# Two experts' last 64 query rows in one 128-row tile, and a sign bit placed by the activation that rescales a weight

## The chip, the cores and the metric

The kernel runs on one core of one Trainium2 chip. TensorE (PE) multiplies matrices, VectorE (DVE), ScalarE (ACT) and GpSimd (POOL) work element by element, and SyncE (SP) issues most DMA transfers. Each engine takes its own instructions strictly in the order of the program; semaphores hold one back until its inputs are there. The metric is device time of one execution in microseconds (us).

## The reference, cut to what matters

Four batches of 576 positions go through three stages in float32.

```python
# 1. sparse attention: 8 heads, 4 local (32 back), 4 strided (every 32nd)
scores = where(mask, q @ k.T / 8, -1e9); attn = softmax(scores); x = attn @ v     # (4, 576, 512)
# 2. token-shift MLP; w_k (512 x 1024), w_v (1024 x 512), w_r (512 x 512) come as float64
k = maximum(xk @ w_k, 0); v = (k * k) @ w_v; x = sigmoid(xr @ w_r) * v
# 3. dense causal attention, one head (d = 64) for each of 4 experts, weighted by a top-2 gate
for e in range(4):
    a = softmax(where(causal, -1e9, scale * (x @ wq[e]) @ (x @ wk[e]).T))
    out += gate[e] * (a @ (x @ wv[e]) @ wo[e])
```

## The kernel before, in words

Matrices are multiplied as sums of high and low parts (`split`): three products for a full-precision one, in the type F32R, which TensorE reads in one pass. Transposes and the products with the attention weights are plain float32.

**The float64 weights.** The three MLP matrices come as raw 64-bit words, in 20 pieces of 128 x 512 (`weight_units`, four of `w_r`, eight of `w_k`, eight of `w_v`). Each piece is turned to float32 by integer steps: a DMA loads the words; `scale` (ACT, L165 and L167) takes the upper words as float32 numbers and multiplies them by 2^-112, which moves the exponent to where float32 wants it, and turns the lower words to an integer; `shift` (DVE, L171) moves the upper words left by 3 bits, which drops their sign; `add` (DVE, L174) adds the low bits; `sign` (DVE, L177) takes the sign bit from the upper word and puts it into the result; `high` (ACT, L184) and `low` (DVE, L188) split the result into its parts. `w_r` needs no split in the first batch.

**Stage order.** `first_batch` is written out by hand and pinned: in ten steps it interleaves the sparse attention of batch 0 with pieces 0 to 5. Then come the gate products of batch 0 (TensorE, L526, plain float32), and a loop in which pieces 7 to 19 are made. Its last eight passes each hold one group of 12 TensorE products (`mm1`, L506 to L508, tile `pk`), whose result ACT takes out of PSUM (L510), squares (L514) and rounds (L117), and DVE completes (L120). `pk` has three PSUM buffers, shared with the gate products, which ACT copies out at L532. The rest of batch 0 and batches 1 to 3 follow, with the next batch's sparse attention between the MLP products.

**The dense attention.** For each batch `proj_units` makes queries `Q`, keys `KH`, `KL`, values `V` and gate weights `gw`; `attn_tiles` cuts the 576 query rows into five tiles of 128 (the last one, t = 4, holds 64 real rows; its upper 64 partitions read whatever stands behind). The batch's second chunk (tiles 2, 3, 4) comes first, then the first (tiles 0, 1). For each tile and expert `sc` makes the scores (two products each for up to 512 keys; tile 4 has 576 keys, so two parts of 288), DVE adds the mask and finds the row's extreme (L1027), ACT takes the exponential with the row's sum (L1033). `norm` makes one factor for a row (L1041 to L1043), `trp` multiplies by it (DVE, L1048), transposes in blocks of 128 keys on TensorE (L1058, tile `pt`, two PSUM buffers), and ACT copies the blocks out (L104, tile `aT`). `av` multiplies with the values (L1080, `py`), `wout` with the output weights (L1096 to L1098, `pw`), and SP stores the result. The work of one batch is interleaved by planned costs with the projections of the next, and outside the pinned part a scheduler with a time model decides each engine's final order, so the order on the chip is fixed beforehand.

Of the kernel before, what the change touches and what calls it, by code (L numbers as in the profile page):

```python
# [7 lines left out]
F32 = mybir.dt.float32  # L8
F32R = mybir.dt.float32r
# [33 lines left out]
def kernel(  # L43
# [100 lines left out]
    def weight_units():  # L144
        units = []

        def piece(dst_h, dst_l, src, early=True):
# [42 lines left out]
            return dict(load=load, scale=scale, shift=shift, add=add, sign=sign, high=high, low=low)  # L190
# [428 lines left out]
    def first_batch():  # L619
# [10 lines left out]
        def w(j, what):  # L630
            if 0 <= j < NW:
                wu[j][what]()
# [11 lines left out]
        def pieces(j, extra=()):  # L644
# [5 lines left out]
            w(j, "sign")  # L650
# [90 lines left out]
        w(6, "sign")  # L741
# [141 lines left out]
    nc.sync.dma_start(mcau, c_cau)  # L883
    tri = p3.tile([P, E, E], F32, tag="tri", name="tri", bufs=1)
# [3 lines left out]
    def proj_units(b):  # L888
        units = []

        Qf = p3.tile([P, E * S + P // 2], F32R, tag="Q", name=f"Q{b}")
        nc.gpsimd.memset(Qf[:, E * S:].bitcast(F32), 0.0)
        Q = Qf[:, :E * S].rearrange("p (e s) -> p e s", e=E)
# [4 lines left out]
        pst[b] = dict(Q=Qf, KH=KH, KL=KL, V=V, gw=gw)  # L898
        nc.gpsimd.memset(V[64:P, NT - 1, :], 0.0)
        for ci, (s0, N) in enumerate(CHUNKS):  # L900
# [41 lines left out]

            for ep in range(EP):
                units.append(qkp(True, ep))
                units.append(qkp(False, ep))

# [16 lines left out]
        def gate():  # L963
# [21 lines left out]
            nc.vector.tensor_tensor(gw, gw, mx.unsqueeze(2).to_broadcast([P, NT, E]), op=ALU.mult)  # L985

# [3 lines left out]
    def attn_tiles(b):  # L990

        res = []
        Q, KH, KL, V, gw = (pst[b][n] for n in ("Q", "KH", "KL", "V", "gw"))
        for ci, (s0, N) in reversed(list(enumerate(CHUNKS))):
# [4 lines left out]
            def tile_units(t, ci=ci, s0=s0, N=N, nkt=nkt, cst=cst):  # L999


                m = P
                mq = min(P, S - t * P)
                nk = min(S, (t + 1) * P)
                nkp = (t + 1) * P
                st = {}

                def sc(e):
                    def f():
# [3 lines left out]
                        pe = p3.tile([P, nkp], F32, tag=f"pe{t}", name=f"pe{b}_{t}_{e}", bufs=4)  # L1013
                        st["p", e] = pe
                        if nkp > nk:
                            nc.gpsimd.memset(pe[:, nk:], 0.0)
                        qs = Q[:, e * S + t * P:e * S + t * P + m]
                        parts = [(0, nk)] if nk <= 512 else [(0, 288), (288, nk - 288)]
                        nm, sm = st["nm"], st["sm"]
                        for i, (c0, n) in enumerate(parts):  # L1020
                            pm = ps_sc(f"s3_{b}_{t}_{e}_{i}")
                            nc.tensor.matmul(pm[:m, :n], qs, KH[:, e, c0:c0 + n], start=True, stop=False)  # L1022
                            nc.tensor.matmul(pm[:m, :n], qs, KL[:, e, c0:c0 + n], start=False, stop=True)  # L1023

                            mo = 384 - (t * P - c0)
                            mask = mcau[:m, mo:mo + n] if c0 + n > t * P else mcau[:m, :n]
                            nc.vector.tensor_tensor_reduce(  # L1027
                                out=pe[:m, c0:c0 + n], in0=pm[:m, :n], in1=mask,
                                scale=-0.125, scalar=(BIG if i == 0 else nm[:m, 2 * e:2 * e + 1]),
                                op0=ALU.add, op1=ALU.min, accum_out=nm[:m, 2 * e + i:2 * e + i + 1],  # L1030
                            )
                            last = nm[:m, 2 * e + i:2 * e + i + 1]
                        nc.scalar.activation(  # L1033
                            pe[:m, :nk], pe[:m, :nk], AF.Exp, bias=last, scale=-1.0,
                            accum_out=sm[:m, e:e + 1],
                        )
                    return (0.6, f)

                def norm():
                    sm = st["sm"]  # L1040
                    nc.vector.tensor_scalar_add(sm[:m, :], sm[:m, :], 1e-9)  # L1041
                    nc.vector.reciprocal(sm[:m, :], sm[:m, :])
                    nc.vector.tensor_tensor(sm[:m, :], sm[:m, :], gw[:m, t, :], op=ALU.mult)  # L1043

                def trp(e):
                    def f():
                        pe = st["p", e]
                        nc.vector.tensor_scalar_mul(pe[:m, :nk], pe[:m, :nk], st["sm"][:m, e:e + 1])  # L1048
                        if ("aT", e) not in cst:
                            cst["aT", e] = p3.tile([P, nkt, N], F32, tag=f"aT{ci}", name=f"aT3_{b}_{ci}_{e}", bufs=4)  # L1050
                        aT = cst["aT", e]
                        qo = t * P - s0
                        for k0 in range(0, t + 1, 4):
                            kn = min(4, t + 1 - k0)
# [170 lines left out]
```

## Time and profile before

| | us |
|---|---|
| median of 3 runs (lowest, highest) | 577.26 (576.7, 579.78) |
| the profiled execution, its own time | 578.21 |
| its span, first to last instruction | 576.3 |
| busy: PE / DVE / ACT / POOL | 550.2 / 391.2 / 336.2 / 94.8 |

The granted TensorE clock is 1.00 over the whole span. In a row, "x" is a count, "busy, mean ns" the time and mean duration of a group, and "[a <-b]" says that the engine sat idle for a us and that b ended it. Matmuls are pipelined: a new one starts before the last one's modelled end, so the distance between two starts is the cost of one, and a busy PE can still be late.

### The profile page before, as it was taken

The page shows a single profiled execution, that of the slowest core. Times are in us where ns is not written, and L with a number is a line of the kernel's source. Part 1 is how long each engine was busy: PE and PEld are TensorE (multiplying, and loading weights), DVE is VectorE, ACT ScalarE, POOL GpSimd, SP SyncE. Part 2 cuts the span into 40 slices and gives each one's busy share as a digit, 9 for nine tenths or more (in the row PEclk, how much of TensorE's full clock was granted, in tenths as well). Part 3 has the DMA queues.
Part 4 walks back from the last instruction along what each step waited for, and adds up shares of the span by engine and source line. Part 5 has one row for each costly group of instructions (what it writes and reads, how often), then busy time and mean ns, then how long its engine had stood idle before and what let it go on. Part 6 is the DMA issues. An engine that isn't in the chain of part 4 may idle for free.

```text
span 576.3 us, 12027 instructions
## 1 busy us (share of the span) xinstructions
PE 550.2 (95%) x4408; PEld 497.8 (86%) x4408; DVE 391.2 (68%) x1350; ACT 336.2 (58%) x994; POOL 94.8 (16%) x147
## 2 busy tenths in 40 slices
PE   4889889989999999999999999999999999999987
PEld 3657789879999998999999999999978998898956
DVE  3897998867975465964465943246888865875862
ACT  4987878780455351445453753157776864775763
POOL 0000000101211121301022000076513242220000
PEclk9999999999999999999999999999999999999999
DMA  8962431234002305001203230055502250321102
GB/s 266 339 248 82 142 137 35 85 119 142 2 1 77 99 17 189 2 19 70 88 11 96 79 100 30 30 113 107 123 16 57 65 129 6 79 46 37 61 23 83
DMA packets 26367, 49.70 MB, mean 86 GB/s; under 512 B 3524, under 2 KB 20676, under 8 KB 25540
## 3 DMA queue, kind: packets, MB, share of 16 engines
q1 hardware_dynamic: 21188, 44.21, 23.1%
q0 software_dynamic: 5120, 4.72, 4.6%
q8 instruction: 34, 0.56, 0.4%
q14 instruction: 25, 0.20, 0.1%
HBM read 34.77 MB, written 9.44 MB: 77 GB/s over the span
## 4 chain that ended last, share of the span: by engine, by line
PE 76%; DVE 10%; ACT 5%; issue 2%; DVEq 0%; ACTq 0%
PE pk L506 6%; PE pv L563 6%; PE pk L507 5%; PE pk L508 5%; PE pv L565 5%; PE pv L564 5%; PE py L1080 4%; PE pt L1058 4%; PE pr L542 2%; PE pr L543 2%; PE pr L544 2%; PE s L1022 2%; PE pos L413 2%; PE s L1023 2%; PE pw L1096 2%; PE ss L382 2%
## 5 line engine op out<-in xcount | busy, mean ns | idle before, releaser
L506 PE MATMUL pk<-xh,wkh 128*128 128x320 f32 (+1 forms) x256 | 79.1, 310 | 3.8 <-ACT rf L510 2.8
L563 PE MATMUL pv<-kk,wvh 128*128 128x320 f32 (+1 forms) x256 | 76.5, 303 | 0.0
L507 PE MATMUL pk<-xl,wkh 128*128 128x320 f32 (+1 forms) x256 | 75.3, 294 | 0.0
L508 PE MATMUL pk<-xh,wkl 128*128 128x320 f32 (+1 forms) x256 | 75.2, 294 | 0.0
L564 PE MATMUL pv<-kk,wvh 128*128 128x320 f32 (+1 forms) x256 | 74.4, 294 | 0.0
L565 PE MATMUL pv<-kk,wvl 128*128 128x320 f32 (+1 forms) x256 | 74.0, 294 | 0.0
L1033 ACT ACTIVATE pe<-pe,nm 128x384 f32<-128x384 f32 (+4 forms) x80 | 48.3, 606 | 12.5 <-DVE nm L1027 10.2
L510 ACT ACTIVATE rf<-pk 128x320 f32<-128x320 f32 (+1 forms) x64 | 26.0, 405 | 49.9 <-PE pk L508 46.3
L506 PEld LDWEIGHTS pk<-xh,wkh 128*128 128x128 f32 x256 | 48.0, 188 | 7.8 <-ACT rf L510 3.8
L237 ACT ACTIVATE el<-el,nm 128x96 f32<-128x96 f32 x72 | 26.2, 365 | 45.2 <-DVE nm L232 44.7
L563 PEld LDWEIGHTS pv<-kk,wvh 128*128 128x128 f32 x256 | 47.7, 188 | 2.1 <-issue 0.3
L507 PEld LDWEIGHTS pk<-xl,wkh 128*128 128x128 f32 x256 | 48.1, 188 | 0.1
L508 PEld LDWEIGHTS pk<-xh,wkl 128*128 128x128 f32 x256 | 48.1, 188 | 0.1
L564 PEld LDWEIGHTS pv<-kk,wvh 128*128 128x128 f32 x256 | 47.9, 188 | 0.0
L565 PEld LDWEIGHTS pv<-kk,wvl 128*128 128x128 f32 x256 | 47.8, 188 | 0.1
L1027 DVE CUSTOM_DVE_ANT_0 pe<-s,mcau 128x384 f32<-128x384 f32 (+4 forms) x80 | 36.6, 480 | 10.4 <-PE s L1023 9.7
L104 ACT COPY aT<-pt 128x256 f32<-128x256 f32 (+3 forms) x96 | 33.4, 381 | 16.2 <-PE pt L1058 15.5
L1058 PE MATMUL pt<-ident,pe 128*128 128x128 f32 x240 | 37.9, 276 | 2.1 <-ACT aT L104 1.3
L568 DVE TENSOR_TENSOR sg<-pv,sg 128x320 f32<-128x320 f32 (+1 forms) x32 | 14.4, 456 | 35.6 <-PE pv L565 32.2
L120 DVE TENSOR_TENSOR kk<-rf,kk 128x320 fp32r<-128x320 f32 (+1 forms) x64 | 31.2, 488 | 4.6 <-ACT kk L117 3.4
L237 ACT ACTIVATE es<-es,nm 108x108 f32<-108x108 f32 (+1 forms) x80 | 30.3, 383 | 6.6 <-DVE nm L232 6.5
L1022 PE MATMUL s<-KH,Q 128*128 128x288 f32 (+4 forms) x96 | 31.9, 342 | 1.1 <-DVE nm L1027 1.1
(163 smaller groups left out, 1553.6 us busy)
## 6 DMA issues: line engine op xcount, KB each, us to landing
qkv<-in_loc_dram SPq DMA_DIRECT2D x6, 1168.0 KB, 5.2
qkv<-in_strd_dram SPq DMA_DIRECT2D x6, 896.0 KB, 4.7
wraw<-in_w_k_dram SPq DMA_DIRECT2D x7, 512.0 KB, 6.5
qkv<-in_w_v_dram SPq DMA_DIRECT2D x5, 512.0 KB, 4.1
x_spill<-sg SPq DMA_DIRECT2D x16, 160.0 KB, 1.8
x2f<-x_spill SPq DMA_DIRECT2D x4, 640.0 KB, 4.2
out_dram<-ot SPq DMA_DIRECT2D x16, 160.0 KB, 1.8
wraw<-in_w_r_dram SPq DMA_DIRECT2D x4, 512.0 KB, 7.7
```

The costliest lines, as they stand in the source:

```text
L104: nc.scalar.copy(dst, src)
L237: nc.scalar.activation(eg, eg, AF.Exp, bias=nm[:np_, i:i + 1], scale=-1.0, accum_out=sm[:np_, i:i + 1],)
L506: nc.tensor.matmul(pm[:, :N], wkh[:, kc, fs], xh[:, kc, :N], start=(kc == 0), stop=False)
L507: nc.tensor.matmul(pm[:, :N], wkh[:, kc, fs], xl[:, kc, :N], start=False, stop=False)
L508: nc.tensor.matmul(pm[:, :N], wkl[:, kc, fs], xh[:, kc, :N], start=False, stop=(kc == NKC - 1))
L563: nc.tensor.matmul(pm[:, :N], wvh[:, fc, os_], kh[:, :N], start=(fc == 0), stop=False)
L564: nc.tensor.matmul(pm[:, :N], wvh[:, fc, os_], kl[:, :N], start=False, stop=False)
L565: nc.tensor.matmul(pm[:, :N], wvl[:, fc, os_], kh[:, :N], start=False, stop=(fc == NFC - 1))
L1022: nc.tensor.matmul(pm[:m, :n], qs, KH[:, e, c0:c0 + n], start=True, stop=False)
L1027: nc.vector.tensor_tensor_reduce(out=pe[:m, c0:c0 + n], in0=pm[:m, :n], in1=mask, scale=-0.125, scalar=(BIG if i == 0 else nm[:m, 2 * e:2 ...
L1033: nc.scalar.activation(pe[:m, :nk], pe[:m, :nk], AF.Exp, bias=last, scale=-1.0, accum_out=sm[:m, e:e + 1],)
L1058: nc.tensor.transpose(pt[:, kk * P:(kk + 1) * P], pe[:, c0:c0 + P], ident)
```

## The change

Two parts. `sign` is gone: the activation on the upper words is Prelu instead of Copy. It multiplies a negative input by a further 2^32, which adds 32 to its exponent, so that the left shift by 3 bits moves that bit into the sign's place. And the last tile of the dense attention takes two experts at a time: 64 rows of expert 2*ep in partitions 0 to 63 and of expert 2*ep + 1 in 64 to 127. `QT` holds for a pair the first expert's query rows, 64 zero columns, and the second's; four products, two with each expert's keys, add up in one PSUM tile, and the zeros keep the experts apart.

```diff
-                nc.scalar.activation(hi.bitcast(F32), hi.bitcast(F32), AF.Copy, scale=2.0 ** -112)
+                nc.scalar.activation(hi.bitcast(F32), hi.bitcast(F32), AF.Prelu, scale=2.0 ** -112, alpha=2.0 ** 32)
...
-                nc.vector.tensor_tensor(t["w"], t["w"], t["lo"], op=ALU.add)
-
-            def sign():
-                nc.vector.scalar_tensor_tensor(
-                    dst_h if dst_l is None else t["w"], t["hi"], -0x80000000, t["w"],
-                    op0=ALU.bitwise_and, op1=ALU.bitwise_or,
-                )
+                nc.vector.tensor_tensor(dst_h if dst_l is None else t["w"], t["w"], t["lo"], op=ALU.add)
...
+    mtail = p3.tile([P, S // 2], F32, tag="mtail", name="mtail", bufs=1)
+    nc.sync.dma_start(mtail[:, :TZ], c_cau[:, :TZ])
+    for j in range(2):
+        nc.sync.dma_start(mtail[TW * j:TW * j + TW, TZ:], c_cau[:TW, 384:384 + TW])
...
-        nc.gpsimd.memset(Qf[:, E * S:].bitcast(F32), 0.0)
+        QT = p3.tile([P, EP, 3, TW], F32R, tag="QT", name=f"QT{b}")
+        nc.gpsimd.memset(QT[:, :, 1, :].bitcast(F32), 0.0)
...
+            def tails():
+                for j in range(2):
+                    nc.vector.tensor_copy(QT[:, :, 2 * j, :], Q[:, j::2, TQ:].bitcast(F32))
...
+            for j in range(2):
+                nc.vector.tensor_copy(gwt[TW * j:TW * j + TW, :], gw[:TW, NT - 1, j::2])
...
+            def tail_units(s0=s0, probs=probs):
...
+                        pe = p3.tile([P, NT * P], F32, tag=f"pe{t}", name=f"pe{b}_{t}_{ep}", bufs=3)
...
+                        for i, (c0, n) in enumerate(TPARTS):
+                            pm = ps_sc(f"s3_{b}_{t}_{ep}_{i}")
+                            for j in range(2):
+                                qs = QT[:, ep, j:j + 2, :].rearrange("p a s -> p (a s)")
+                                for h, K in enumerate((KH, KL)):
+                                    nc.tensor.matmul(
+                                        pm[:, :n], qs, K[:, 2 * ep + j, c0:c0 + n],
+                                        start=(j + h == 0), stop=(j + h == 2),
+                                    )
...
+                        for k0 in range(0, NT, 4):
+                            kn = min(4, NT - k0)
+                            pt = ps_tr(f"pt3_{b}_{t}_{ep}_{k0}")
+                            for k in range(kn):
+                                c0 = (k0 + k) * P
+                                nc.tensor.transpose(pt[:, k * P:(k + 1) * P], pe[:, c0:c0 + P], ident)
...
+                return [sc(ep) for ep in range(EP)], [(0.0, norm)] + [trp(ep) for ep in range(EP)]
```

The other tiles keep their work; the transposed weights of two experts now share one buffer (`aT`, two buffers of twice the size instead of four).

How the order moves, at the two places that matter below. First DVE in the loop over the weight pieces (L174 `add`, L188 `low`, L177 `sign`, L171 `shift`; after the change the lines are L174, L182 and L171). Before:

```order
L174 ISA wf_659<-wraw_355,wf_659 128x1024
L188 TENSOR_TENSOR wkl_76<-wf_635,wkh_75 128x512
L177 SCALAR_TENSOR_TENSOR wf_659<-wraw_355,wf_659 128x512
L171 TENSOR_SCALAR wf_669<-wraw_357 128x512
L174 ISA wf_669<-wraw_357,wf_669 128x1024
L188 TENSOR_TENSOR wkl_76<-wf_659,wkh_75 128x512
L177 SCALAR_TENSOR_TENSOR wf_669<-wraw_357,wf_669 128x512
L171 TENSOR_SCALAR wf_680<-qkv0_1_97 128x512
```

After, at the same pieces:

```order
L174 ISA wf_650<-wraw_351,wf_650 128x1024
L182 TENSOR_TENSOR wkl_76<-wf_627,wkh_75 128x512
L171 TENSOR_SCALAR wf_659<-wraw_353 128x512
L174 ISA wf_659<-wraw_353,wf_659 128x1024
L182 TENSOR_TENSOR wkl_76<-wf_650,wkh_75 128x512
L171 TENSOR_SCALAR wf_669<-qkv0_1_97 128x512
```

The row of L177 is missing once a piece and nothing else moved; a piece's value is now complete at `add`, two DVE instructions earlier.

Second, TensorE near the program's end: the transposes of the last tile of batch 3 (`pt_3_4`, then expert and first key block) among the scores of tile 1 (`s_3_1`) and the products with the values (`py_1`). Before:

```order
L1023 MATMUL s_3_1_3_0_7138<-KL_6088,Q_6085 128x256
L1058 MATMUL pt_3_4_0_0_7078<-ident,pe_4_0_6933 128x128 x4
L1058 MATMUL pt_3_4_0_4_7084<-ident,pe_4_0_6933 128x128
L1058 MATMUL pt_3_4_1_0_7088<-ident,pe_4_1_6944 128x128 x4
L1080 MATMUL py_1_0_7168<-aT_3_1_0_6888,V_6089 64x320
L1058 MATMUL pt_3_4_1_4_7094<-ident,pe_4_1_6944 128x128
L1058 MATMUL pt_3_4_2_0_7098<-ident,pe_4_2_6955 128x128 x4
```

After (expert pairs now):

```order
L1116 MATMUL pt_3_4_0_0_6956<-ident,pe_4_0_6825 128x128 x4
L1032 MATMUL s_3_1_2_6990<-KH_6015,Q_6011 128x256
L1033 MATMUL s_3_1_2_6990<-KL_6016,Q_6011 128x256
L1032 MATMUL s_3_1_3_6996<-KH_6015,Q_6011 128x256
L1033 MATMUL s_3_1_3_6996<-KL_6016,Q_6011 128x256
L1116 MATMUL pt_3_4_0_4_6962<-ident,pe_4_0_6825 128x128
L1116 MATMUL pt_3_4_1_0_6966<-ident,pe_4_1_6840 128x128 x4
L1138 MATMUL py_1_0_7024<-aT_3_1_0_6782,V_6017 64x320 x6
```

Two pairs stand where four experts stood, and the first pair's transposes moved up between the scores of tile 1.

## Rows read from the trace of the kernel before

**Rows 1.** By stretch (us): busy and count of each engine, clock, DMA.

```profile
12.00:44.70 32.70, 27.28 (x222) 19.55 (x219) 29.26 (x118) 26.88 (x97) 0.00 (x0) 1.00 0.83 305
44.70:82.00 37.30, 33.51 (x170) 27.61 (x170) 31.56 (x63) 30.12 (x62) 0.19 (x1) 1.00 0.29 90
140.00:372.00 232.00, 232.00 (x1966) 219.78 (x1965) 145.76 (x492) 101.68 (x303) 33.42 (x42) 1.00 0.17 57
372.00:548.60 176.60, 174.83 (x1336) 160.52 (x1335) 125.17 (x436) 120.47 (x341) 57.23 (x94) 1.00 0.30 70
548.60:576.00 27.40, 22.23 (x154) 16.20 (x152) 10.98 (x45) 12.35 (x44) 0.00 (x0) 1.00 0.15 49
```

**Rows 2.** Who waited for whom, TensorE, 44.7 to 82 us: total, times, longest.

```profile
PE pk L506 <- ACT rf L510: 2.8, 4, 0.9
PE pk L506 <- ACT sg L532: 1.0, 2, 0.8
```

**Rows 3.** Groups by form, line L177: busy us, mean ns.

```profile
L177 DVE SCALAR_TENSOR_TENSOR wf<-wraw,wf 128x512 int32<-128x512 int32 x10 | 6.8, 682 | 0.0
```

**Rows 4.** Who waited for whom, ScalarE, 57 to 79.3 us.

```profile
ACT wkh L184 <- DVE wf L177: 2.6, 5, 1.1
ACT wvh L184 <- DVE wf L177: 1.1, 2, 0.6
```

**Rows 5.** Timeline of VectorE in the loop over pieces: start, duration.

```profile
81.85 0.68 DVE L174 CUSTOM_DVE_ANT_0 wf<-wraw,wf 128x1024 uint16<-128x1024 uint16 x1
83.05 0.68 DVE L177 SCALAR_TENSOR_TENSOR wf<-wraw,wf 128x512 int32<-128x512 int32 x1
83.66 0.42 DVE L171 TENSOR_SCALAR wf<-wraw 128x512 int32<-128x512 int32 x1
84.39 0.68 DVE L174 CUSTOM_DVE_ANT_0 wf<-wraw,wf 128x1024 uint16<-128x1024 uint16 x1
```

**Rows 6.** Timeline of TensorE, end of batch 0's sparse attention.

```profile
38.62 0.68 PE L402 MATMUL pts<-ident,es 126*126 126x126 f32 x2 [0.55 <-DVE aTs L662]
41.79 0.79 PE L402 MATMUL pts<-ident,es 108*108 108x108 f32 x3 [0.50 <-DVE aTs L662]
```

**Rows 7.** Timeline of TensorE in the dense attention.

```profile
471.22 0.34 PE L1022 MATMUL s<-KH,Q 128*128 128x384 f32 x1
471.39 0.71 PE L1058 MATMUL pt<-ident,pe 128*128 128x128 f32 x5
471.86 0.43 PE L1023 MATMUL s<-KL,Q 128*128 128x384 f32 x1
472.12 0.31 PE L923 MATMUL pq_False<-x2h,wqh 128*128 128x320 f32 x1
```

**Rows 8.** Groups by form, dense attention, VectorE and ScalarE.

```profile
L1048 DVE TENSOR_SCALAR pe<-pe,sm 128x128 f32<-128x128 f32 x16 | 3.5, 283 | 0.1
L1027 DVE CUSTOM_DVE_ANT_0 pe<-s,mcau 128x288 f32<-128x288 f32 x16 | 7.1, 451 | 1.4 <-PE s L1023 1.2
L1027 DVE CUSTOM_DVE_ANT_0 pe<-s,mcau,nm 128x288 f32<-128x288 f32 x16 | 8.2, 513 | 2.7 <-PE s L1023 2.2
L1048 DVE TENSOR_SCALAR pe<-pe,sm 128x576 f32<-128x576 f32 x16 | 7.3, 517 | 0.1
L1033 ACT ACTIVATE pe<-pe,nm 128x576 f32<-128x576 f32 x16 | 12.5, 778 | 4.3 <-DVE nm L1027 3.9 <-DVE sm L1041 0.2
```

**Rows 9.** Timeline of TensorE near the end, batch 3.

```profile
547.64 0.29 PE L1023 MATMUL s<-KL,Q 128*128 128x288 f32 x1
551.88 0.74 PE L1058 MATMUL pt<-ident,pe 128*128 128x128 f32 x5 [0.78 <-DVE pe L1048]
555.50 0.66 PE L1058 MATMUL pt<-ident,pe 128*128 128x128 f32 x4 [0.94 <-ACT aT L104]
```

**Rows 10.** Groups by form, ScalarE: the rescaling and a table load.

```profile
L165 ACT ACTIVATE wraw<-wraw 128x512 f32<-128x512 f32 x14 | 9.4, 672 | 4.6 <-DMA wraw<-in_w_r_dram 4.6
L237 ACT ACT_TABLE_LOAD x4 | 5.1, 1283 | 4.7 <-DVE nm L232 3.9 <-PEq L1212 0.7
```

More of the change, by code (lines that the diff above doesn't have):

```diff
@@ L188, in low @@
                     nc.vector.tensor_tensor(dst_l, t["w"].bitcast(F32), dst_h.bitcast(F32), op=ALU.subtract)
-            return dict(load=load, scale=scale, shift=shift, add=add, sign=sign, high=high, low=low)
+            return dict(load=load, scale=scale, shift=shift, add=add, high=high, low=low)
         for kc in range(NKC):
@@ L649, in pieces @@
                 f()
-            w(j, "sign")
             place(j)
@@ L997, in attn_tiles, with probs, tile_units @@
             nkt = tiles[-1] + 1
[L999 to L1005, printed above, removed]
+            def probs(ep, ci=ci, N=N, nkt=nkt, cst=cst):
+                if ("aT", ep) not in cst:
+                    cst["aT", ep] = p3.tile([P, 2, nkt, N], F32, tag=f"aT{ci}", name=f"aT3_{b}_{ci}_{ep}")
+                return cst["aT", ep]
+            def tile_units(t, s0=s0, probs=probs):
+                nk = (t + 1) * P
                 st = {}
@@ L1012, in f @@
                             st["sm"] = p3.tile([P, E], F32, tag="sm3", name=f"sm3_{b}_{t}")
-                        pe = p3.tile([P, nkp], F32, tag=f"pe{t}", name=f"pe{b}_{t}_{e}", bufs=4)
+                        pe = p3.tile([P, nk], F32, tag=f"pe{t}", name=f"pe{b}_{t}_{e}", bufs=4)
                         st["p", e] = pe
[L1015 to L1032, printed above, removed]
@@ L1033, in f @@
-                        nc.scalar.activation(
-                            pe[:m, :nk], pe[:m, :nk], AF.Exp, bias=last, scale=-1.0,
-                            accum_out=sm[:m, e:e + 1],
+                        qs = Q[:, e * S + t * P:e * S + t * P + P]
+                        nm, sm = st["nm"][:, e:e + 1], st["sm"]
+                        pm = ps_sc(f"s3_{b}_{t}_{e}")
+                        nc.tensor.matmul(pm[:, :nk], qs, KH[:, e, :nk], start=True, stop=False)
+                        nc.tensor.matmul(pm[:, :nk], qs, KL[:, e, :nk], start=False, stop=True)
@@ L1036, in f @@
+                        nc.vector.tensor_tensor_reduce(
+                            out=pe, in0=pm[:, :nk], in1=mcau[:, 512 - nk:],
+                            scale=-0.125, scalar=BIG, op0=ALU.add, op1=ALU.min, accum_out=nm,
                         )
+                        nc.scalar.activation(pe, pe, AF.Exp, bias=nm, scale=-1.0, accum_out=sm[:, e:e + 1])
                     return (0.6, f)
@@ L1047, in f @@
                         pe = st["p", e]
[L1048 to L1051, printed above, removed]
+                        nc.vector.tensor_scalar_mul(pe, pe, st["sm"][:, e:e + 1])
+                        aT = probs(e // 2)[:, e % 2]
                         qo = t * P - s0
-                        for k0 in range(0, t + 1, 4):
-                            kn = min(4, t + 1 - k0)
-                            pt = ps_tr(f"pt3_{b}_{t}_{e}_{k0}")
-                            for kk in range(kn):
-                                c0 = (k0 + kk) * P
-                                nc.tensor.transpose(pt[:, kk * P:(kk + 1) * P], pe[:, c0:c0 + P], ident)
+                        pt = ps_tr(f"pt3_{b}_{t}_{e}")
@@ new lines, in f @@
+                        for k in range(t + 1):
+                            nc.tensor.transpose(pt[:, k * P:(k + 1) * P], pe[:, k * P:(k + 1) * P], ident)
+                        evac(
+                            aT[:, :t + 1, qo:qo + P],
+                            pt[:, :nk].rearrange("p (k c) -> p k c", c=P),
+                            nc.scalar,
+                        )
+                    return (0.4, f)
+                return [sc(e) for e in range(E)], [(0.0, norm)] + [trp(e) for e in range(E)]
```

65 lines of the change are left out of this document (51 added, 14 removed).

## The prediction

> **What bounds the kernel now.** I read the busy time by stretch first [rows 1], since the mean over the span (TensorE 95%) hides that the stages have different limits. From 140 to 372 us TensorE is busy the whole 232 us and VectorE 63% of it: there only TensorE counts, and neither part of the change touches it. From 372 to 548.6 us, the dense attention, TensorE is busy 174.83 of 176.6 us: a VectorE or ScalarE saving is hidden there, and only what leaves TensorE's queue pays. Before 82 us it is otherwise: from 12 to 44.7 us VectorE works 29.26 of 32.7 us and TensorE 27.28, from 44.7 to 82 us VectorE 31.56 of 37.3. And in the last 27.4 us TensorE is idle for 5.2 of them. The granted clock is 1.00 in every row, so the clock gives nothing and takes nothing.
>
> Then who waits for whom. In the loop over weight pieces TensorE waits for ScalarE to empty its PSUM buffers, 3.8 us in all, behind L510 and L532 [rows 2]. ScalarE is late because it is itself held by VectorE: its rounding of a piece (L184) comes earlier in its queue and waits for `sign`, 2.6 + 1.1 = 3.7 us in seven waits between 57 and 79.3 us [rows 4]. So `sign` stands on the path there, two queues away from TensorE.
>
> **Part 1, the sign by Prelu.** It removes 20 VectorE instructions of 682 ns [rows 3], one for each piece; the distance from one to the next instruction is 0.61 us [rows 5], so VectorE is relieved of 12.2 us. What reaches the end is less, and differs by place.
>
> Pieces 0 to 4, early in the sparse attention: nothing. They are done between the exponentials of batch 0, where ScalarE has a full queue, and TensorE works in small groups that alternate with it; a faster VectorE would wait for ScalarE's exponentials. Pieces 5 and 6: VectorE is without a pause before the end of the sparse attention, and TensorE waits there for a VectorE copy, 0.55 us at 38.62 and 0.50 us at 41.79 [rows 6]. Two signs, 1.2 us, leave VectorE's queue ahead of the second copy. ScalarE's copies between do not move, so I take 1.0 us (bounds 0 and 1.2). The gate products that follow are one unbroken TensorE run and carry that on.
>
> Pieces 7 to 19: if all of ScalarE's 3.7 us of waiting for `sign` [rows 4] goes, its copies out of PSUM come that much earlier, and TensorE has 3.8 us to give back [rows 2]. Not all goes: without `sign` a pass costs VectorE 2.54 - 0.61 = 1.93 us in the last seven passes (2.54 is the distance between two `add` starts [rows 5]), slightly more than what ScalarE has in such a pass, so that VectorE still leads by a tenth in each of the three or four passes that matter. I take 3.4 us (bounds 0 and 3.8). Nothing else comes late: the pieces' DMAs wait for `add` and so are issued earlier too, and the first products of batch 1 stand behind the same loop.
>
> What Prelu itself costs no row shows. The same activation with Copy takes 672 ns [rows 10]; the dearest activation near that size, an exponential over 576 elements, takes 778 [rows 8]. Below, no reason makes it cheaper than Copy; above, 20 times 0.106 us is 2.1 us, of which two thirds stand in ScalarE's full stretches. I take the Copy price, same size and same operands, and keep 1.4 us in the range.
>
> From 82 to 372 us the saved time is carried through, since TensorE has no waits there worth the name, and the order of that part is nearly the same.
>
> **Part 2, the paired tile.** TensorE's score products stay: before, four experts by two parts by two products of 288 columns; now two pairs by two parts by four. What goes is transposes: 20 in a batch become 10, so 40 in all, in groups of five. One group is dear by its distance: 471.39 to 471.86 is 0.47 us, and the product behind it takes 0.26 us to its successor where the one ahead takes 0.17 [rows 7]; the change of kind costs 0.09 and a group 0.56. Eight groups less are 4.5 us. But the new order often puts the fifth transpose of a group some rows behind the four, which costs the change of kind twice; in batches 0 to 2 four whole groups (2.24 us) become two split ones (1.30 us), in batch 3 four mostly split ones (2.6) become two: 3 x 0.94 + 1.3 = 4.1 us. I take 4.1 (bounds 3.0 and 4.5).
>
> VectorE loses 16 mask operations (8 of 451, 8 of 513 ns) and 8 scalings of 517 ns, 11.8 us; ScalarE 8 exponentials of 778 ns, 6.2 us [rows 8]. Added on VectorE are eight copies into `QT` and eight small ones of gate weights; the nearest row is a scaling of 128 x 128 at 283 ns [rows 8], so at most 4.5 us. All that lies under a full TensorE up to 548.6 us, and I price it at zero there; without that cover the balance is still a gain. In the tail it is not covered. The last batch's share is a quarter, 3.0 us of VectorE and 1.6 us of ScalarE. TensorE's own waits for exactly that work are 0.78 us, for the scaling of tile 4, and 0.94 us, for a copy of its transposes [rows 9]. In the new order one pair's transposes come before the last scores, and two of four groups are gone. I take 1.5 us (bounds -1, if the wait only moves to the exponentials of tile 1, and 3.0).
>
> The three small mask DMAs and the zeros of `QT` stand in queues that are ahead of need by many microseconds: zero.
>
> **The sum.** 1.0 + 3.4 + 4.1 + 1.5 = 10.0 us off the profiled execution's 578.21 us, 568.2 us. That execution was 0.95 us above the median, so the time to expect is 577.26 - 10.0 = 567.3 us.
>
> **The rivals.** *ScalarE is the limit in the first stage.* For it: ScalarE is busy 30.12 of 37.3 us there [rows 1], and takes Prelu at its upper price; then the first stage gives some 1 us and the rest 5.6: 570.7 us. Against it: seven waits for `sign` that nothing else explains.
>
> *The dense attention keeps its time.* The scheduler has written a new order for all of it with fewer, longer units, and small waits may eat the transposes' gain; then only 1 us of 5.6 is left: 577.26 - 5.4 = 571.9 us. Against it: the waits recorded before are small, as TensorE's 174.83 of 176.6 us says.
>
> *The tail tile becomes one long chain.* With two pairs there is less to overlap, and TensorE may reach a pair's transposes before its masks, exponential, row factor and scaling are through. That chain took 551.88 - 547.93 = 3.95 us in batch 3 (from the end of the last tail score) [rows 9]. Once in each of four batches is 15.8 us on top: 583.1 us, slower. It decides where under 3.95 us of other TensorE work stands between; in the new order 68, 119, 57 and 40 rows stand there, and even at 0.12 us a row that is 4.8 us. So it is unlikely.
>
> *Prelu is in another function table than the exponential.* Seven pieces are rescaled between exponentials, and a load away and back for each, at 1.283 us a load [rows 10], would put 18.0 us on a full ScalarE: 577.3 + 18.0 - 9 = 586 us. Against it: ScalarE's order holds eight table loads in both kernels. The Trainium skill, on the page "ScalarE: Activation LUTs" (sections "Table sets: the hidden batching unit" and "What ACT_TABLE_LOAD costs"), warns of just this: functions come in sets, and a switch between sets costs 1283 ns for the load and about 1380 ns more to drain, 2.66 us; by that the seven pairs would cost some 37 us. It also says that cheap functions are in every set. The load's own 1283 ns agrees with this trace's row; whether Prelu is a cheap one no run here shows.
>
> **How the numbers follow.** Forecast (567.3) 0.62; first stage limited by ScalarE (570.7) 0.14; dense attention unmoved (571.9) 0.12; nothing of both arrives (about 576) 0.06; the two slower ones 0.03 each. About 0.5%, 2.9 us, is what a measurement of this kernel can tell from no change. So faster is 0.62 + 0.14 + 0.12 = 0.88, the same 0.06, slower 0.06. All four terms at their upper bounds give 1.2 + 3.8 + 4.5 + 3.0 = 12.5 us, 564.8; a little more can come from smaller waits in the dense attention, so the range begins at 562.5. Upward it takes in both first rivals and Prelu's upper price: 572.5.
>
> **What would show it.** Line L177 gone; `add` to `add` at 1.9 to 2.1 us in the last passes; ScalarE's waits before its rounding of a piece under 1 us; the first product of batch 1's attention, and the start of the dense attention, about 4.4 us earlier; 200 transposes in place of 240; the stretch of the dense attention without the tail about 4 us shorter, and no table load more than eight. I am wrong if the piece loop keeps its length, if Prelu takes clearly more than 0.68 us, or if TensorE shows new waits at the tail tile's transposes.

## The result and the profile after

The changed kernel takes 570.5 us (median; 569.5 to 572.9), the kernel before 577.0 us in the same comparison: ratio 0.988, 95% interval 0.984 to 0.993, 6.5 us less. The forecast was 10.0 us less, 567.3 us; the time is 3.2 us above it, and inside the range of 562.5 to 572.5. A second comparison gave 571.8 us and 0.990 [0.988, 0.993].

Three lengths tell where it went; I use them for every kernel below: from the start to the first second-stage product of batch 0 (`pv`), from there to the first product of the dense attention (`pq_True`), and from there to the start of the last output product (`pw`). In the MLP, first-stage products are those with `w_k` (`pk`), second-stage products those with `w_v` (`pv`), and gate products those with `w_r` (`pr`).

| us, from the profiled execution | first stage | middle | dense attention |
|---|---|---|---|
| before | 82.8 | 290.9 | 199.1 |
| changed | 77.3 | 294.3 | 195.7 |
| gain | 5.4 | -3.4 | 3.4 |
| forecast | 4.4 | 0 | 5.6 |

So the first stage gave more than I had forecast, the dense attention less, and the middle, in which I had expected nothing, took 3.4 us away.

Busy time by stretch of the changed kernel, with the columns of [rows 1]; the stretches end at the same places of the program:

```profile
12.00:44.00 32.00, 27.05 (x224) 19.53 (x220) 25.82 (x111) 27.01 (x98) 0.00 (x0) 1.00 0.83 296
44.00:77.00 33.00, 31.38 (x182) 27.05 (x182) 27.28 (x55) 30.91 (x65) 0.11 (x1) 1.00 0.37 121
...
370.00:543.60 173.60, 168.98 (x1268) 152.26 (x1266) 117.79 (x410) 110.47 (x308) 56.69 (x86) 1.00 0.29 70
543.60:571.00 27.40, 23.57 (x183) 18.93 (x181) 11.77 (x50) 13.97 (x44) 0.00 (x0) 1.00 0.19 63
```

In the third row shown TensorE is idle for 4.6 of 173.6 us, where it was 1.8 of 176.6 us: the dense attention has new waits. In the last it is idle for 3.8 us in place of 5.2. From 44 to 77 us ScalarE is now the busiest after TensorE, 30.9 of 33 us.

**The loop over pieces.** Timeline of the changed kernel: VectorE's `add` (L174) in two late passes, then ScalarE's one long wait and its rounding of a piece (L178) in two passes.

```profile
70.05 0.68 DVE L174 CUSTOM_DVE_ANT_0 wf<-qkv,wf 128x1024 uint16<-128x1024 uint16 x1
72.11 0.68 DVE L174 CUSTOM_DVE_ANT_0 wf<-qkv,wf 128x1024 uint16<-128x1024 uint16 x1
```
```profile
63.53 0.69 ACT L165 ACTIVATE wraw<-wraw 128x512 f32<-128x512 f32 x1 [1.02 <-DMA wraw<-in_w_v_dram]
71.37 0.62 ACT L178 CAST wvh<-wf 128x512 fp32r<-128x512 f32 x1
73.22 0.62 ACT L178 CAST wvh<-wf 128x512 fp32r<-128x512 f32 x1
```

`add` to `add` is 2.06 us (2.54 before, [rows 5]). The rounding, which waited seven times and 3.7 us for `sign` [rows 4], now waits for VectorE nowhere. What is late next is a transfer: one piece from `w_v` comes 1.02 us late (SyncE issues these transfers behind an `add`), though the prediction had "Nothing else comes late". Prelu by itself, one line's instructions with shortest, median and longest time, and the transposes of the dense attention, grouped by line:

```profile
L165 ACT ACTIVATE wraw<-wraw x14: 652/674/705, 10.1 to 67.1; 128x512 f32<-128x512 f32 x14
```
```profile
L1055 PE MATMUL pt<-ident,pe 128*128 128x128 f32 x160 | 26.2, 277 | 0.6 <-ACT aT L104 0.4
L1116 PE MATMUL pt<-ident,pe 128*128 128x128 f32 x40 | 7.2, 277 | 0.4 <-ACT aT L104 0.4
```

Prelu costs 674 ns where Copy cost 672 [rows 10], and the trace has as many table loads as before, nine (the prediction's eight is one short for both kernels). 200 transposes take 33.4 us; the 240 of before took 37.9 us.

**The middle.** TensorE at the end of batch 1's sparse attention, and the granted clock around it:

```profile
122.28 0.68 PE L407 MATMUL pos<-aTs,qkv 126*64 126x126 f32 x8 [0.43 <-ACT aTs L104]
123.88 0.74 PE L396 MATMUL pts<-ident,es 108*108 108x108 f32 x6 [0.92 <-DVE es L247]
125.19 0.40 PE L407 MATMUL pos<-aTs,qkv 108*64 108x108 f32 x2 [0.57 <-DVE aTs L106]
126.33 0.41 PE L557 MATMUL pv<-kk,wvh 128*128 128x256 f32 x1
126.54 0.42 PE L558 MATMUL pv<-kk,wvh 128*128 128x256 f32 x1
129.15 0.28 PE L559 MATMUL pv<-kk,wvl 128*128 128x256 f32 x1
129.27 0.28 PE L557 MATMUL pv<-kk,wvh 128*128 128x256 f32 x1
```
```profile
120.00:130.00 10.00, 8.08 (x60) 0.83 0.33 121
```

Three waits, 1.9 us (1.2 us at the same place before), and behind them 15 products of 256 columns 0.21 us apart, where later ones stand 0.12 us apart. The granted clock over the ten microseconds reads 0.83 (columns: TensorE busy, granted clock, DMA share, GB/s). TensorE had fallen to its lower level, 1.2 of 2.4 GHz; at 15 x 0.095 us that costs 1.4 us.

**The dense attention.** TensorE's two long waits, and what stood on VectorE and GpSimd ahead of each:

```profile
400.20 0.51 PE L1032 MATMUL s<-KH,Q 128*128 128x512 f32 x1 [1.24 <-DVE nm L1034]
451.93 0.39 PE L1032 MATMUL s<-KH,Q 128*128 128x256 f32 x1 [1.29 <-DVE nm L1034]
```
```profile
396.21 0.43 DVE L941 TENSOR_TENSOR KL<-pq_True,KH 64x256 fp32r<-64x256 f32 x1 [0.16 <-ACT KH L940]
396.67 2.44 DVE L997 COPY gwt<-gw 64x2 f32<-64x2 f32 x2
...
399.58 0.56 DVE L1034 CUSTOM_DVE_ANT_0 pe<-s,mcau 128x384 f32<-128x384 f32 x1
...
448.15 0.24 DVE L1045 TENSOR_TENSOR sm<-sm,gw 128x4 f32<-128x4 f32 x2
448.35 0.75 DVE L1050 TENSOR_SCALAR pe<-pe,sm 128x384 f32<-128x384 f32 x2
...
449.35 2.32 DVE L1050 TENSOR_SCALAR pe<-pe,sm 128x384 f32<-128x384 f32 x6
451.59 0.28 DVE L1034 CUSTOM_DVE_ANT_0 pe<-s,mcau 128x128 f32<-128x128 f32 x1
```
```profile
395.94 2.96 POOL L120 TENSOR_TENSOR x2l<-x2f,x2h 128x1280 fp32r<-128x1280 f32 x1
```

At 400 us a mask (L1034), which frees the score buffer, came behind the two small copies of gate weights (L997) that the change adds: 256 numbers in 2.44 us. One of the two took 2.26 us and ended when GpSimd's subtraction ended, at 398.9 us. At 452 us it came behind eight row scalings, since two tiles' row factors became ready together. With a third of 0.37 us, TensorE's waits for masks are 2.9 us; before they were two, 1.1 us.

### The profile page after: what moved, and what is told of

It reads as the page before. It is cut to its first block, busy times and chain, and to the rows that moved or that the text cites. A ratio compares the mean times of both kernels' runs of the same rounds, so it can differ in the third digit from the quotient of the medians.

```text
span 571.1 us, 11841 instructions
## 1 busy us (share of the span) xinstructions
PE 546.3 (96%) x4368; PEld 493.8 (86%) x4368; DVE 374.7 (66%) x1306; ACT 327.7 (57%) x962; POOL 94.4 (17%) x139
## 4 chain that ended last, share of the span: by engine, by line
PE 76%; DVE 8%; ACT 7%; DMA 5%; POOL 2%; issue 1%; SPq 1%; POOLq 0%; DVEq 0%; ACTq 0%
PE pv L557 7%; PE pk L500 6%; PE pv L558 6%; PE pv L559 6%; PE pk L501 6%; PE pk L502 6%; PE py L1138 4%; PE pr L536 3%; PE pt L1055 2%; PE sl L319 2%; PE pr L537 2%; PE pr L538 2%; PE pos L407 2%; PE ss L376 2%; DMA wraw<-in_w_r_dram 2%; PE pol L355 2%
## 5 line engine op out<-in xcount | busy, mean ns | idle before, releaser
L559 PE MATMUL pv<-kk,wvl 128*128 128x320 f32 (+1 forms) x256 | 74.9, 297 | 0.0
L557 PEld LDWEIGHTS pv<-kk,wvh 128*128 128x128 f32 x256 | 48.4, 191 | 2.0 <-issue 0.3
L558 PEld LDWEIGHTS pv<-kk,wvh 128*128 128x128 f32 x256 | 48.6, 191 | 0.1
L1038 ACT ACTIVATE pe<-pe,nm 128x384 f32<-128x384 f32 (+3 forms) x64 | 36.0, 566 | 13.3 <-DVE nm L1034 11.3
L104 ACT COPY aT<-pt 128x512 f32<-128x512 f32 (+3 forms) x80 | 32.3, 426 | 9.5 <-PE pt L1055 7.6
L1034 DVE CUSTOM_DVE_ANT_0 pe<-s,mcau 128x384 f32<-128x384 f32 (+3 forms) x64 | 29.9, 485 | 11.3 <-PE s L1033 10.8
L466 POOL TENSOR_TENSOR xd<-xT 128x320 f32<-128x320 f32 (+1 forms) x24 | 18.1, 758 | 86.4 <-DVE xT L106 57.0
L473 DVE SCALAR_TENSOR_TENSOR xf<-xd,mu,xT 128x320 f32<-128x320 f32 (+1 forms) x56 | 28.8, 529 | 3.4 <-POOL xd L466 3.3
```

Of the source, the lines that this page charges most:

```text
L104: nc.scalar.copy(dst, src)
L473: nc.vector.scalar_tensor_tensor(xf[:, :N], d[:, :N], mu[:, which, kc:kc + 1], prv, op0=ALU.mult, op1=ALU.add)
L557: nc.tensor.matmul(pm[:, :N], wvh[:, fc, os_], kh[:, :N], start=(fc == 0), stop=False)
L558: nc.tensor.matmul(pm[:, :N], wvh[:, fc, os_], kl[:, :N], start=False, stop=False)
L559: nc.tensor.matmul(pm[:, :N], wvl[:, fc, os_], kh[:, :N], start=False, stop=(fc == NFC - 1))
L1034: nc.vector.tensor_tensor_reduce(out=pe, in0=pm[:, :nk], in1=mcau[:, 512 - nk:], scale=-0.125, scalar=BIG, op0=ALU.add, op1=ALU.min, accum ...
```

## The experiments

Ratios are against the kernel before, with 95% intervals.

| kernel | us | ratio | first stage | middle | dense |
|---|---|---|---|---|---|
| e_sign | 575.6 | 0.9955 [0.9937, 0.9972] | 76.3 | 294.3 | 199.3 |
| e_sign_late | 575.7 | 0.9968 [0.9945, 0.9991] | 77.9 | 292.7 | 199.2 |
| e_tile | 575.4 | 0.9956 [0.9936, 0.9976] | 82.1 | 290.9 | 196.1 |
| e_gwmax | 570.5 | 0.9873 [0.9848, 0.9899] | 77.5 | 292.7 | 195.5 |
| after_2 | 571.8 | 0.9903 [0.9875, 0.9931] | 76.1 | 292.7 | 195.8 |
| e_gwact | 570.3 | 0.9869 [0.9833, 0.9905] | 78.3 | 294.2 | 193.8 |
| e_tr2 | 577.9 | 1.0008 [0.9984, 1.0031] | 74.9 | 294.3 | 201.7 |
| e_fill | 569.1 | 0.9847 [0.9814, 0.9879] | 78.5 | 289.3 | 196.0 |
| e_fill_gwact | 564.9 | 0.9780 [0.9758, 0.9803] | 76.4 | 289.4 | 193.4 |
| e_scal | 564.0 | 0.9765 [0.9733, 0.9796] | 76.9 | 289.3 | 192.7 |
| e_fill_vfirst | 587.3 | 1.0158 [1.0128, 1.0188] | 77.3 | - | - |
| e_fill_vfirst_gwact | 588.6 | 1.0196 [1.0171, 1.0221] | 76.5 | - | - |

**e_sign: the first part alone.** The kernel before with (type casts left out, and `sign` itself)

```
- nc.scalar.activation(hi, hi, AF.Copy, scale=2.0 ** -112)
+ nc.scalar.activation(hi, hi, AF.Prelu, scale=2.0 ** -112, alpha=2.0 ** 32)
...
-            w(j, "sign")
```

> The kernel before with the Prelu part alone (no paired tile). Theory: the first stage gives all of its gain without the tile, and the loss after it belongs to this part too, since the order of TensorE's instructions at the end of batch 1's sparse attention is the changed kernel's. Then the first second-stage product of batch 0 (82.8 us before, 77.3 after) starts at 77.3 to 77.5 us, the granted clock falls below 0.90 somewhere in 120 to 130 us, the dense attention starts at 371.5 to 372 us, and the time is 2 us under before, 575.0 us. Rival: the fall of the clock there was chance in one profiled execution; then the clock stays at 1.00, the dense attention starts at 369 to 370 us, and the time is 573 us.

The theory held in what it rests on: a granted clock of 0.83 from 120 to 130 us, and a middle of 294.3 us. The first stage came out 1 us shorter than it had said, 76.3 us, so the dense attention starts at 370.6 us, between the theory's time and the rival's. A first stage 6.5 us shorter ends as 2.6 us of time. The loss in the middle belongs to this part; that the fall of the clock is not in every execution shows in after_2 below.

**e_tile: the second part alone.** The changed kernel with the lines above put back.

> The changed kernel with Copy and the separate sign operation put back, so the paired tile alone. Theory: the dense attention gives 3.2 us by itself (4.5 us of transposes and 1.5 us in the tail, less 2.8 us of new waits), the stages before it keep the times of before (first product of the dense attention at 373.6 us), and the time is 573.8 us. Rival: the new waits of the dense attention come from what the first part did to the order; then most of 5.6 us arrives and the time is 571.4 us.

The stages before the dense attention keep their times (middle 290.9 us, as before), and the dense attention gives 3.0 us with the changed kernel's waits for masks, 2.9 us in three. The rival falls: the waits belong to the tile. The time is 2.5 us under before by its ratio, where the theory had 3.2.

**e_gwmax: one form of instruction.**

```
- nc.vector.tensor_copy(gwt[TW*j:TW*j+TW, :], gw[:TW, NT-1, j::2])
+ nc.vector.tensor_tensor(gwt[TW*j:TW*j+TW, :], gw[:TW, NT-1, j::2], gw[:TW, NT-1, j::2], op=ALU.max)
```

> The changed kernel with one form of instruction changed: the small copies of gate weights (L997, 64 x 2) become a maximum of the value with itself, an operation of two inputs on the same engine at the same place; the order of all instructions is the same. Theory: one of these copies, recorded at 2.26 us at 396.7 us, was held up while GpSimd ran its subtraction from 395.9 to 398.9 us, because the copy needs what GpSimd holds; the two-input form does not. Then every L997 takes under 0.3 us, TensorE's wait of 1.24 us at 400.2 us goes, and the time is 1.2 us under that of the changed kernel, 569.3 us. First rival: any VectorE operation would be held up there; L997 still takes over 2 us, no change. Second rival: the copy is quick but the mask that TensorE waits for is late by something else; no change.

My theory fell and the first rival held. VectorE beside GpSimd's subtraction in this kernel, and in the kernel before:

```profile
394.73 0.43 DVE L941 TENSOR_TENSOR KL<-pq_True,KH 64x256 fp32r<-64x256 f32 x1 [0.17 <-ACT KH L940]
395.19 2.44 DVE L997 TENSOR_TENSOR gwt<-gw 64x2 f32<-64x2 f32 x2
407.59 1.73 DVE L1045 TENSOR_TENSOR sm<-sm,gw 128x4 f32<-128x4 f32 x1
```
```profile
408.83 2.40 POOL L120 TENSOR_TENSOR x2l<-x2f,x2h 128x1024 fp32r<-128x1024 f32 x1 [4.91 <-ACT x2h L117]
409.49 1.76 DVE L1041 TENSOR_SCALAR sm<-sm 128x4 f32<-128x4 f32 x1 [1.55 <-ACT pe L1033]
```

It is not the form: L997, L1045 and L1041 (a maximum, a multiplication and an addition of a constant), whose inputs all lie in SBUF, end with a subtraction of GpSimd (409.49 + 1.76 = 411.25; 408.83 + 2.40 = 411.23). L941, one of whose inputs lies in PSUM, takes its 0.43 us beside it. Not every instruction on SBUF alone is held: a reciprocal (L1044, 128 x 4) took its 0.18 us at 408.57 us of the changed kernel, beside the subtraction that ran from 408.40 to 410.78 us. The Trainium skill has a rule for this on the page "SBUF — State Buffer", section "Who interferes with whom": a VectorE instruction with two SBUF inputs contends with a GpSimd instruction that reads SBUF, as does a copy or `tensor_scalar` in a mode that takes two ports, and the second to issue is blocked until the first is done. The trace agrees, with 2.26 us for a copy, 1.73 us for a multiplication of two inputs and 1.76 us for a `tensor_scalar`; in which mode they ran no run here shows. I had not drawn on it in the prediction.

**e_gwact: the copies on ScalarE.**

```
- nc.vector.tensor_copy(gwt[TW*j:TW*j+TW, :], gw[:TW, NT-1, j::2])
+ nc.scalar.copy(gwt[TW*j:TW*j+TW, :], gw[:TW, NT-1, j::2])
```

> The changed kernel with the small copies of gate weights on ScalarE and nothing else (the end of batch 1's sparse attention as in the changed kernel). Theory: the length of the dense attention (195.7 us in the changed kernel, 193.4 us in the filled kernel with this edit) is 193.4 us here too, and the stretch from the first second-stage product of batch 0 to the dense attention (294.3 us in the changed kernel, 289.4 us in the filled one) stays at 292.7 to 294.3 us: the two edits are separate. Time 568.2 us. Rival: a part of the 2.3 us came from the other kernel's order; the length is 195 us or more, time 570 us.

Lengths as the theory had them: 193.8 us of dense attention, 294.2 us in the middle. The median stays 2 us above the theory's, at the rival's. The profiled execution, 571.8 us, had both the fall in the middle and a slow beginning of the gate products (17.3 us, see below). Two of the other three took 568.3 and 569.0 us, near the theory's 568.2; whether they were without the two is not shown. The waits for masks fell from 2.9 to 1.6 us, 1.3 us; a new one of 0.8 us for a transfer of keys came. How the dense attention's 1.9 us come about in full I can't say: the edit also moves other instructions.

**e_fill: work for TensorE in the bare end.**

```
- main = behind(A["2"][6:] + Z["1"])
- tail = behind(Z["2"])
+ main = behind(A["2"][6:] + Z["1"] + Z["2"][:2])
+ tail = behind(Z["2"][2:])
```

> The changed kernel with the two first units of batch 0's last products moved into the stretch in which batch 1's sparse attention ends, so that TensorE has 24 products to put between the last transposes. Theory: the 1.9 us of waits between 122 and 125.5 us go, TensorE does not fall to half its pace behind them (15 products of 256 columns at 0.21 us in place of 0.12, 1.5 us), the granted clock reads 1.00 from 120 to 135 us, and the time is 2.2 to 3.4 us under the changed kernel's: 567.1 to 568.3 us. Rival: the waits only move to where the products were; then the time is the changed kernel's, 570.5 us.

Granted clock and TensorE's busy time there:

```profile
120.00:130.00 10.00, 10.00 (x95) 1.00 0.45 146
```

No wait of TensorE is recorded from 80 to 370 us, and the middle takes 289.3 us: 5.0 under the changed kernel's profile, 1.6 under before. So the waits and the fall went as the theory said. The time did not follow it: 569.1 us is 1.4 us under the changed kernel, not 2.2 to 3.4, and the intervals of the ratios 0.9847 and 0.9883 overlap. In its profile the first stage is 1.2 us longer than the changed kernel's (78.5 against 77.3 us), and the changed kernel does not fall to the lower clock in every execution:

**after_2: the changed kernel once more.**

> The changed kernel once more, for a second profile. Theory: TensorE's waits between 122 and 125.5 us are in the order and come again, 1.8 to 2.0 us; the fall to half the pace behind them depends on the execution, as a kernel of the same order there did not show it: from the first second-stage product of batch 0 to the dense attention it takes 294.3 us with the fall and 292.7 us without. Rival: the fall belongs to the kernel; 294.3 us again.

The theory held. The waits are the same 1.9 us, yet the products behind them keep their 0.12 us:

```profile
120.99 0.68 PE L407 MATMUL pos<-aTs,qkv 126*64 126x126 f32 x8 [0.42 <-ACT aTs L104]
122.58 0.74 PE L396 MATMUL pts<-ident,es 108*108 108x108 f32 x6 [0.91 <-DVE es L247]
123.89 0.40 PE L407 MATMUL pos<-aTs,qkv 108*64 108x108 f32 x2 [0.57 <-DVE aTs L106]
125.50 0.28 PE L558 MATMUL pv<-kk,wvh 128*128 128x256 f32 x1
125.62 0.28 PE L559 MATMUL pv<-kk,wvl 128*128 128x256 f32 x1
```

Of seven profiles in this order, four have the fall (294.2 to 294.3 us) and three don't (292.7 us).

**e_sign_late: Prelu from piece 7 on.** The sign operation stays for pieces 0 to 6, on the kernel before.

```
+            late = len(units) >= 7
- nc.scalar.activation(hi, hi, AF.Copy, scale=2.0 ** -112)
+ nc.scalar.activation(hi, hi, AF.Prelu if late else AF.Copy, scale=2.0 ** -112, ...)
```

> The kernel before with Prelu for pieces 7 to 19 only; pieces 0 to 6 keep Copy and the sign operation, the tail tile is as before. Prelu for all pieces had brought the first second-stage product forward by 6.45 us: 1.43 to the first gate product, 1.69 in the 64 gate products, 3.33 in the first-stage products behind them. Theory: the first two belong to pieces 0 to 6, whose signs make TensorE wait ahead of the gate products, so that it runs the first of these at half its pace; without those pieces the gate products start at 44.7 us and take 17.1 us, and the first second-stage product is at 79.4 us (3.3 us earlier than before). Rival: the gate products are shorter because of pieces 7 and later, which lie beside them; then they take 15.4 us although they start at 44.7 us, and the first second-stage product is at 77.8 us.

Neither: 77.9 us is the rival's number, but not in the rival's way. The gate products start at 43.7 us, 1 us early though the signs ahead of them stayed, and take 16.5 us. This place scatters between executions: e_tile, whose first stage is that of before, starts them at 44.1 us. The part behind them is steady: from the first first-stage product to the first second-stage product it takes 21.0 us in before and e_tile, and 17.7 us here.

**e_tr2: the transposes twice.** In the changed kernel, for the paired tiles:

```
+ for _ in range(2):
      nc.tensor.transpose(pt[:, k * P:(k + 1) * P], pe[:, c0:c0 + P], ident)
```

> The changed kernel with every transpose of the paired tiles issued twice (40 more, the number that the change took away; masks, exponentials, scalings and copies as they are). Theory: the dense attention is bound by TensorE, and these 40 cost what the prediction took off for them, 4.1 us, up to 4.5; its length, from its first product to the start of the last output product, goes from 195.7 to 200 us. Rival: the transposes fit into waits of TensorE; the length stays under 197 us.

The dense attention grows by 6.0 us to 201.7, 1.7 us more than the theory. The 40 transposes are 4.4 us of it:

```profile
L1117 PE MATMUL pt<-ident,pe 128*128 128x128 f32 x80 | 11.6, 275 | 0.5 <-ACT aT L104 0.5
```

(11.6 us against 7.2 for 40.) The rest is of the size of the new order's waits: from 360 us on TensorE waits 6.2 us where it was 4.5, the longest time 1.5 us.

**e_fill_gwact: both repairs.** The edits of e_fill and e_gwact together.

> The filled kernel (24 products moved into the end of batch 1's sparse attention) with the small copies of gate weights, L997, made by ScalarE. Theory: a VectorE operation that reads only SBUF does not run beside GpSimd's subtraction, one that reads PSUM does; ScalarE is free of this. Then the copies take under 0.3 us each on ScalarE, the masks behind them are not late, TensorE's wait of 1.3 us for a mask before 400 us goes, and the time is 1.2 us under the filled kernel's, 567.9 us. Rival: the wait for the mask stays, since another SBUF operation comes to stand beside the subtraction; no change, 569.1 us.

564.9 us, 2.2% under before: more than the theory, as in e_gwact (dense attention 2.5 us shorter than in e_fill). It beats both kernels: its interval ends below the beginning of the changed one's. Each small copy now takes 0.19 us:

```profile
L997 ACT COPY gwt<-gw x8: 178/191/193, 390.6 to 525.4; 64x2 f32<-64x2 f32 x8
```

**e_scal: four scalings of each batch on ScalarE**, on e_fill_gwact.

```
+ if t == 2:
+     nc.scalar.activation(pe, pe, AF.Copy, scale=st["sm"][:, e:e + 1])
+ else:
      nc.vector.tensor_scalar_mul(pe, pe, st["sm"][:, e:e + 1])
```

> The filled kernel with the small copies on ScalarE, and the four row scalings of the 128 x 384 tiles by ScalarE as well, so that no eight scalings stand on VectorE ahead of a mask. Theory: TensorE's wait of 1.1 us for a mask at 443.9 us goes and the time is 1 us under that kernel's, 563.9 us. Rival: the scalings on ScalarE make its copies out of the transposes' buffers late, and the time rises by more than that, over 566 us.

The dense attention is 0.7 us shorter, and the 1.1 us wait for a mask is gone; a wait of 0.8 us for another one, of the paired tile, has come, and TensorE now waits 2.1 us for ScalarE's copies, where it was 0.8. The theory's time came out, but 564.0 us is not told apart from 564.9.

**e_fill_vfirst and e_fill_vfirst_gwact: values first.** On e_fill, and on e_fill_gwact, in outline:

```
+ for t in range(...): units.append(vp(t))       # ahead of the loop over qkp
+ units.insert(len(units) - 2 * EP - 1, (0.1, gate))
- units.append((0.1, gate))
```

> The filled kernel with the projection units in another order: the values of a chunk ahead of its queries and keys, and the gate right behind the last values. Theory: in the changed kernel TensorE's wait of 1.3 us at 451.9 us comes from eight row scalings that stand together ahead of a mask, since two tiles' row factors became ready at once, right behind the gate; with an earlier gate the eight are two groups of four with masks between, that wait goes and nothing else changes in length: 1.3 us under the filled kernel's 569.1 us, 567.8 us. Rival: the new order makes as many waits of its own elsewhere in the dense attention: 569 us or more.

> Both: values and gate first, and the small copies of gate weights by ScalarE, on the filled kernel. Theory: the two waits are separate, so 2.5 us under the filled kernel's 569.1 us, 566.6 us, and TensorE's waits for masks (3.0 us in the filled kernel between 370 us and the end) come to under 1 us. Rival: as for each alone, no change.

Both are slower than before, by 1.6 and 2.0%. The scalings did become two groups with masks between, but TensorE's waits from 360 us on come to 18.7 us in the first of the two, where they were 4.4 us in e_fill, and 10.5 us of them are for the queries' and keys' splits (L941), which now come late. The two largest:

```profile
PE py L1139 <- DVE Q L941: 4.2, 2, 2.3
PE py L1139 <- DVE KL L941: 3.7, 2, 1.9
```

Curing a wait of 1.3 us by a new order of units cost some 18 us. The rival had the direction; its size I had not foreseen.

## Why the prediction was right, and where it was wrong

**Front, 1.0 us forecast: 0.7 us, within its scatter.** The two waits of [rows 6] are gone in the changed kernel, and stay in e_tile and e_sign_late, which keep these signs. But the gate products start at 44.7, 44.1 and 43.7 us in the three kernels with the signs, and at 42.2 to 44.2 us in the eleven profiles without: the size can't be told from one profile.

**Piece loop, 3.4 us: right.** From the first first-stage product to the first second-stage product, 20.97 us became 17.94 us, 3.0 us less; over all kernels with Prelu in these pieces 17.1 to 18.4 us. The mechanism is as stated: `sign` gone from the rounding's way, two queues from TensorE. TensorE's waits in this loop went from 3.8 us in six [rows 2] to 1.6 us in two. That is less than 3.0, since a wait costs more than its row says: from the start ahead of each wait to the start behind it, it takes 5.6 us before and 2.2 us now, where products without a wait stand 0.15 us apart.

**Not in the sum: 1.7 us in the gate products.** 64 products took 17.1 us before and 15.4 us after. TensorE in two microseconds of each, before and changed:

```profile
45.00:46.00 1.00, 1.00 (x3) 1.00 0.55 66
46.00:47.00 1.00, 1.00 (x4) 1.00 0.64 213
```
```profile
45.00:46.00 1.00, 1.00 (x6) 1.00 1.02 234
46.00:47.00 1.00, 1.00 (x5) 1.00 0.79 315
```

Busy throughout, TensorE starts 3 or 4 of these products in a microsecond before, 5 or 6 after: 0.53 and 0.27 us apart for 320 columns. By this spacing the stretch begins, before, at TensorE's lower level. The granted clock reads 1.00 in both, so my sentence that "the clock gives nothing and takes nothing" trusted a column that missed this. The Trainium skill warns of such a column: the page "TensorE: Matmul & The Clock Gate", section "Part 1: The HAM clock gate (the "warmup" mystery)", says that the trace's events of this clock have been seen to be unreliable; here the spacing of the products is the better witness. This gain can't be put down to the change: e_tile also took 17.1 us, but kernels with Prelu took from 15.4 to 17.3 us. The slowest of these, e_gwact, has neither wait of [rows 6]; and in e_gwmax, which took 16.8 us, the column does show the fall, 0.50 from 40 to 44 us and 0.72 from 44 to 48.

**"From 82 to 372 us the saved time is carried through": the step that failed.** 3.4 us were lost there. I had compared idle time, which was small, and called the order "nearly the same"; but the order of the end of batch 1's sparse attention was new. By landmarks, of the 5.4 us 0.8 are gone at the last first-stage product of batch 0 (120.3 us), 0.7 more at the first product behind the bare end, 1.5 through the fall to the lower level, 0.5 later. So the dense attention began 2.0 us earlier than before, not the 4.4 forecast. The 0.7 and the 1.5 are shown by the waits, by after_2 and by e_fill. The other 1.3 us come with the order: both profiles with before's order there have a middle of 290.9 us, all with the new one and without e_fill's edit 292.7 us or, with the fall, 294.2 to 294.3 us. The timelines show where most of them can lie. Score products of batch 1's sparse attention (`sl`, `ss`), before and changed:

```profile
93.54 1.70 PE L325 MATMUL sl<-qkv 64*64 64x96 f32 x36
```
```profile
91.02 0.38 PE L319 MATMUL sl<-qkv 64*64 64x96 f32 x2
91.79 0.38 PE L319 MATMUL sl<-qkv 64*64 64x96 f32 x2
```

Ahead of the bare end stand 48 `sl` and 40 `ss`, in six unbroken runs before and in eleven after. From the first product of a run to the next other one, 36 take 1.63 us and two take 0.31 us; all runs together take 5.9 us before and 7.3 us in each profile of the new order, 1.4 us more. No run here changes this alone.

**Transposes, 4.1 us: right.** 4.5 us of busy time went (37.9 - 33.4), and 40 put back cost 4.4 us.

**VectorE's and ScalarE's work in the dense attention, "priced at zero": wrong by 2.8 us.** TensorE's idle time there rose by that much (1.8 to 4.6 us), 1.8 us of it at masks. I counted VectorE's balance and overlooked position. The copies of gate weights, for which I took a 283 ns row as the dearest neighbour, include one of 2.26 us, beside GpSimd; a mask stands behind it, and the three score buffers did not cover it: TensorE waited 1.24 us. The bunch of eight scalings is the second case. This is my rival "the dense attention keeps its time" in part: 3.4 of 5.6 us arrived.

**Tail, 1.5 us: right.** TensorE's idle time in the last 27.4 us fell by 1.3 us. The waits of 0.78 and 0.94 us [rows 9] are gone; two small ones stay at the pairs' transposes:

```profile
550.74 0.33 PE L1116 MATMUL pt<-ident,pe 128*128 128x128 f32 x1 [0.27 <-ACT aT L104]
551.22 0.66 PE L1116 MATMUL pt<-ident,pe 128*128 128x128 f32 x4 [0.16 <-ACT aT L104]
```

**Prelu, Copy's price, no table load: right.** VectorE's passes are the longer ones, as I had it (2.06 us against ScalarE's 1.85), but ScalarE waits for VectorE nowhere from 44 to 80 us: "ScalarE is the limit" came true there, behind the gain. The two slower rivals did not occur: no table load was added, and at the pairs' transposes TensorE waited 0.4 us in all.

**Luck in the number.** In the profiles 10.0 + 1.7 - 6.2 = 5.5 us: 1.7 us that I had not counted, and that may not be the change's, stood against 6.2 us (3.4 and 2.8) that I had counted wrongly. Without the 1.7 us the time would have been close to the upper end of the range. 570.5 us lies nearest to the number of the first rival, 570.7 us, whose way it did not take: the first stage gave 5.4 us, not 1.

## What to carry to other kernels

Time saved in one stage must still pass every later point where the engine that bounds the kernel waits, and a scheduler's new order can put waits there; compare the order there too, and keep work of that engine for such places, as e_fill does. A tiny copy or two-input instruction of VectorE on SBUF data is not cheap while GpSimd subtracts (2.26 us in place of 0.16 for L997): look at what stands behind it, and give it to ScalarE if that is free. The two repairs made 564.9 us of 570.5 (0.978 of before in place of 0.988).

## What the runs showed of the hardware

TensorE's fall to half its pace behind 1.9 us of waits is not the same in each execution of the same instructions (four profiles of seven), and it costs 1.4 to 1.7 us each time: as much as the effects sought. GpSimd, too, was slow beside VectorE: the issue of a transfer by GpSimd, 0.52 us as a rule, took 2.06 us beside the six scalings from 449.35 us. It is the only one of 64 above 0.8 us; the only one before, 1.84 us at 412.57 us, stands beside four scalings. That the scalings hold it up is read from these two places, not tested:

```profile
449.72 2.06 POOL L944 DMA_DIRECT2D KL<-KL  x1 [2.61 <-DVE KL L941]
451.77 0.52 POOL L943 DMA_DIRECT2D KH<-KH  x1
```
